# The three remaining slabs of the first x tile in one DMA transpose, ahead of W1's later blocks

## The chip, the cores and the metric

The kernel runs on one core of a Trainium2 chip. The metric is the device time of one execution in microseconds (us), the median of the runs. Before the change it is 212.85 us over 3 runs.

## The reference

Two branches over the same input x (2048 x 640, bf16) are mixed by a gate:

```
g = sigmoid(sum(x * gate_w))                 # one gate for each row
a = 2 * Re(h C^T) + x * Dskip,  h[t] = Lam_bar * h[t-1] + B_bar x[t]   # complex state, 640 wide
b = gelu(x w1 + b1) w2 + b2                  # 640 -> 1728 -> 640
out = g * a + (1 - g) * b
```

The change concerns the first product of branch b alone, x w1, for the first 512 rows of x.

## The kernel before

x is worked on in four tiles of 512 rows. TensorE sums over the partition dimension, so each tile is needed transposed: `xT[q]` holds five slabs of 128 columns of x, each as 128 partitions x 512 rows. W1 lies in `W1sb` as five blocks of 128 rows (block k goes with slab k). Its first 1,024 columns (`FW`, eight groups of 128) are loaded block by block, the other 704 columns for all blocks at once, in two remainders (`w1_r0`, `w1_r1`).

The program isn't written in the order in which it runs. Each piece of work is an `op` with an engine, an estimated duration and latency, and a priority. `Sched.order` then gives every engine a fixed list: at each step it takes, among the items whose inputs are there by the estimates, the one with the lowest priority number. Loads without inputs go to the sync queue (SP) strictly by priority. `Emitter` puts semaphore waits in front of the items that need them.

The start of the kernel, which the change touches, goes like this on the sync queue (priority in brackets):

- `xna0`, `xna1` (0, 0.2): the first two slabs' worth of x, untransposed, 128 KB each. TensorE transposes them through PSUM (L428) and VectorE copies them to slabs 0 and 1 of `xT[0]` (L434).
- W1 block 1 (1) and block 2 (4), 256 KB each (L333, in `load`). Block 0 comes on ScalarE's queue.
- `xtrans(0, 2..2)` (5): slab 2 by a DMA transpose out of x (L340, in `load_T`).
- W1 block 3 (6), `xtrans(0, 3..4)` (7): slabs 3 and 4 in one DMA transpose, W1 block 4 (8).
- the remainders of W1 (20, 21), then the DMA transposes of B (30 to 31.1), of the second x tile (32) and so on.

On TensorE, `m1_first` (L650) makes the product of the first tile with the first 1,024 columns, slab by slab instead of column group by column group, so that it can begin with slab 0 while the others are still on their way. Eight PSUM banks hold the sums. Its order is slab 0 for groups 0 to 6, slab 1 for groups 0 to 6, slab 2 for groups 0 to 6, then the held-back group 7 of slabs 0, 1 and 2, then slabs 3 and 4. A small transpose of the rows of parameters (`cols`, L455) comes between slabs 1 and 2. A matmul of slab k waits for slab k and for block k of W1:

```
                op(f"m1_0_{jf}_{k}_{t0}", "pe", d_mm(t1 - t0), (XK0[k] if h is None else XK0[k][h:h + 1]) + [w1tok(k, jf)], [("bank", jf)],
                   f_mm, prio=pe_prio())
```

All slabs that come by one DMA transpose share one semaphore. Behind `m1_first` follow the rest of the first product (L672, which needs the remainders), the product with B (L715), and the other tiles.

Of the kernel before, what the change touches and what calls it, by code (L numbers as in the profile page):

```python
# [184 lines left out]
def bass_gated_mix__ssm_conv_s5__dense_activation_gelu__prompt_kernel(  # L185
# [22 lines left out]
    KD = D // 128  # L208
# [17 lines left out]
    with ExitStack() as es:  # L226
# [103 lines left out]
        def load(name, eng, sem, dst, src, writes, prio, dur=0.5, lat=2.5, reads=(), after=()):  # L330
            def fn():
                with nc.allow_non_contiguous_dma(reason="columns of small vectors"):
                    return dma_inc(eng, engines[eng].dma_start(dst, src), sem)  # L333
            return op(name, eng, dur, reads, writes, fn, prio=prio, lat=lat, after=after)

        def load_T(name, sem, pairs, writes, prio, dur, lat=3.0, reads=()):
            def fn():
                t = None
                for dst, src in pairs:
                    t = dma_inc("sp", nc.sync.dma_start_transpose(dst, src), sem)  # L340
                return t
            return op(name, "sp", dur, reads, writes, fn, prio=prio, lat=lat)
# [10 lines left out]
        def xtrans(q, ks, prio, dur):  # L353
            load_T(f"xT{q}_{ks[0]}", f"l_xT{q}_{ks[0]}", [(xT[q][:, ks[0]:ks[-1] + 1, :], x2[q * 512:(q + 1) * 512, ks[0] * 128:(ks[-1] + 1) * 128])],
                   [("xT", q, k) for k in ks], prio, dur)
# [3 lines left out]
        def w1load(k, eng, prio, reads=()):  # L359
            edges = [0] + ([WSPLIT[k] * 128] if k in WSPLIT else []) + [FW]  # L360
            for i, (f0, f1) in enumerate(zip(edges, edges[1:])):
                load(f"w1_{k}{i}", eng, f"l_w1{k}{i}", W1sb[:, k, f0:f1], B_w1[k * 128:(k + 1) * 128, f0:f1], [("w1", k, i)], prio=prio + 0.1 * i, lat=2.6, reads=reads)
# [4 lines left out]
        KN = 2  # L367
# [2 lines left out]
            load(f"xna{h}", "sp", f"l_xna{h}", xn[0][:, 2 * h:2 * h + 2, 0:KN * 128],  # L370
                 x2[h * 256:(h + 1) * 256, 0:KN * 128].rearrange("(c p) d -> p c d", p=128), [("xna", h)], 0.2 * h, dur=0.45, lat=2.0 + 0.4 * h)
        w1load(1, "sp", 1)
        w1load(2, "sp", 4)
        xtrans(0, range(2, 3), 5, 1.15)
        w1load(3, "sp", 6)
        xtrans(0, range(3, 5), 7, 1.8)
        w1load(4, "sp", 8)
        FM = FW + 3 * 128
        for i, (f0, f1) in enumerate(((FW, FM), (FM, F))):
            load(f"w1_r{i}", "sp", f"l_w1r{i}", W1sb[:, :, f0:f1], B_w1[:, f0:f1].rearrange("(k p) f -> p k f", p=128), [("w1", "r", i)], prio=20 + i, lat=5.0)  # L380
# [723 lines left out]
```

## Time and profile before

| | us |
|---|---|
| median of 3 runs | 212.85 (212.7 to 212.89) |
| the profiled execution's own time | 212.76 |
| its span, first to last instruction | 211.4 |
| TensorE busy | 207.8 (98% of the span) |
| VectorE busy | 190.1 (90%) |
| ScalarE busy | 103.2 (49%) |

The mean granted TensorE clock is 1.000. All times of instructions are counted from the span's start. PE is a TensorE matmul, PEld a TensorE weight load, DVE VectorE, ACT ScalarE, SP the sync engine, SPq an instruction that its sequencer runs (a DMA issue, whose time is that of the issue, not of the transfer). L340 is line 340 of the kernel. A transfer "lands" when its semaphore has got the full count; the answers on DMA issues give the time from the start of the issue to the landing.

### The profile page before, as it was taken

To read this page: it belongs to the slowest core of one execution; us is meant where nothing else is said; L and a number is where in the kernel's file an instruction comes from. 1 tells how busy PE (TensorE), PEld (TensorE's weight loads), DVE (VectorE), ACT (ScalarE), POOL (GpSimd) and SP (SyncE) were. 2 spreads that over 40 slices of the span, in tenths; PEclk is the share of its full clock that TensorE was granted. 3 is DMA by queue.
4 is the path that set the end of the run, shared out by engine and by line. 5 is a ranking of instruction groups with operands and counts; after the bars stand their busy time and mean duration, and the time that the engine had idled before them with its cause. 6 is when DMAs were issued, how large, how long until landed. Compare 5 with 4: busy or idle time off the path is not lost.

```text
span 211.4 us, 2742 instructions
## 1 busy us (share of the span) xinstructions
PE 207.8 (98%) x1091; PEld 105.3 (50%) x1106; DVE 190.1 (90%) x240; ACT 103.2 (49%) x177; POOL 4.2 (2%) x12
## 2 busy tenths in 40 slices
PE   8999999999999999999999999999999999999996
PEld 4544444444564444444464444444456444567775
DVE  2499999999999999999999999899999999499744
ACT  2399556679850353556680063456660037623330
POOL 1000000120000000000100000000010000000000
DMA  6999899999400020066174000007642000005251
GB/s 177 285 222 152 207 192 249 337 168 222 112 0 3 0 50 0 0 87 147 18 59 115 3 0 0 0 2 77 139 96 112 0 3 0 0 0 105 67 142 62
DMA packets 48504, 19.08 MB, mean 90 GB/s; under 512 B 41452, under 2 KB 47212, under 8 KB 48492
## 3 DMA queue, kind: packets, MB, share of 16 engines
q1 hardware_dynamic: 46688, 17.33, 38.4%
q0 software_dynamic: 1600, 1.32, 4.6%
q10 hardware_dynamic: 204, 0.27, 0.5%
q8 instruction: 8, 0.13, 0.3%
q14 instruction: 4, 0.03, 0.1%
HBM read 8.41 MB, written 2.63 MB: 52 GB/s over the span
## 4 chain that ended last, share of the span: by engine, by line
PE 98%; issue 0%; DVE 0%
PE ps L672 22%; PE ps L715 20%; PE ps L939 20%; PE ps L988 15%; PE ps L802 7%; PE ps L851 5%; PE ps L650 4%; PE ps L416 1%; PE ps L693 1%; PE ps L950 1%; PE ps L428 0%; PE ps L816 0%; DVE W1sb L885 0%; PE ps L441 0%; PE ps L455 0%
## 5 line engine op out<-in xcount | busy, mean ns | idle before, releaser
L672 PE MATMUL ps<-xT,W1sb 128*128 128x512 bf16 x214 | 47.5, 379 | 0.3
L755 DVE TENSOR_TENSOR_SCAN W<-atab,V 128x1280 bf16<-128x1280 f32 x16 | 44.3, 2812 | 0.3
L715 PE MATMUL ps<-xT,BT 128*128 128x512 bf16 x196 | 43.3, 379 | 0.2
L939 PE MATMUL ps<-Gl,W2sb 128*128 128x512 bf16 (+1 forms) x230 | 42.3, 343 | 0.2
L679 ACT ACTIVATE Gl<-ps,cols 128x512 bf16<-128x512 f32 x44 | 29.8, 695 | 15.5 <-PE ps L672 15.5
L672 PEld LDWEIGHTS ps<-xT,W1sb 128*128 128x128 bf16 x220 | 21.5, 98 | 25.9
L988 PE MATMUL ps<-Hb,CT 128*128 128x512 bf16 x150 | 32.9, 379 | 0.0
L939 PEld LDWEIGHTS ps<-Gl,W2sb 128*128 128x128 bf16 x234 | 22.9, 98 | 19.3
L715 PEld LDWEIGHTS ps<-xT,BT 128*128 128x128 bf16 x200 | 19.5, 98 | 23.8 <-ACT Gt L701 0.4
L724 ACT ACTIVATE U<-ps 128x512 bf16<-128x512 f32 x40 | 23.7, 596 | 15.5 <-PE ps L715 15.5
L957 ACT ACTIVATE E1T<-ps,cols 128x512 bf16<-128x512 f32 (+1 forms) x18 | 9.4, 624 | 36.0 <-PE ps L950 36.0
L988 PEld LDWEIGHTS ps<-Hb,CT 128*128 128x128 bf16 x150 | 14.4, 98 | 17.9 <-issue 0.6
L996 ACT ACTIVATE E2T<-ps 128x512 bf16<-128x512 f32 x15 | 9.1, 604 | 13.6 <-PE ps L988 13.6
L802 PE MATMUL ps<-W2sb,Gl 128*128 128x320 bf16 x104 | 14.8, 299 | 0.0
L624 DVE SCALAR_TENSOR_TENSOR trf<-xn,gwb 128x640 bf16<-128x640 bf16 x16 | 13.2, 822 | 0.4
L505 DVE TENSOR_TENSOR V<-V,W 128x1280 bf16<-128x1280 bf16 x16 | 12.5, 821 | 0.3
L505 DVE TENSOR_TENSOR Hb<-Hb,V 128x1280 bf16<-128x1280 bf16 x16 | 12.5, 821 | 0.3
L505 DVE TENSOR_TENSOR V<-mr,U 128x2560 bf16<-128x2560 bf16 x8 | 11.9, 1492 | 0.3
L802 PEld LDWEIGHTS ps<-W2sb,Gl 128*128 128x128 bf16 x104 | 10.1, 98 | 4.3 <-issue 0.3
L505 DVE TENSOR_TENSOR Hb<-c,W 128x2560 bf16<-128x2560 bf16 x8 | 11.9, 1490 | 0.2
L505 DVE TENSOR_TENSOR W<-mi,U 128x2560 bf16<-128x2560 bf16 x8 | 11.9, 1484 | 0.0
L505 DVE TENSOR_TENSOR V<-s,W 128x2560 bf16<-128x2560 bf16 x8 | 11.9, 1484 | 0.0
(93 smaller groups left out, 152.0 us busy)
## 6 DMA issues: line engine op xcount, KB each, us to landing
W2sb<-in_B_w_dram SPq DMA_DIRECT2D x1, 2080.0 KB, 8.7
out_dram<-xn SPq DMA_DIRECT2D x3, 640.0 KB, 4.8
xn<-in_A_x_dram POOLq DMA_DIRECT2D x2, 640.0 KB, 7.4
W1sb<-in_B_w_dram SPq DMA_DIRECT2D x4, 256.0 KB, 4.1
trf<-grow SPq DMA_DIRECT2D x3, 256.0 KB, 5.6
xn<-in_A_x_dram SPq DMA_DIRECT2D x1, 640.0 KB, 7.0
W1sb<-in_B_w_dram SPq DMA_DIRECT2D x1, 480.0 KB, 5.4
out_dram<-W1sb SPq DMA_DIRECT2D x3, 160.0 KB, 1.8
```

The source lines that it names most:

```text
L505: return inc("dve", nc.vector.tensor_tensor(out=o, in0=a, in1=b, op=o_))
L624: t = inc("dve", nc.vector.scalar_tensor_tensor(out=scr[:, :], in0=xn[q % 2][:, c, :], scalar=1.0, in1=gwb[:, :], op0=ALU.mult, op1=ALU.mu ...
L672: t = nc.tensor.matmul(PS[bank][:, :], W1sb[:, k, jf * 128:(jf + 1) * 128], xT[q][:, k, :], start=(k == 0), stop=(k == KD - 1))
L679: return inc("act", nc.scalar.activation(Gl[q % 2][:, jf, :], PS[bank][:, :], ACT.Gelu_apprx_tanh, bias=b1col[:, jf:jf + 1]))
L715: t = nc.tensor.matmul(PS[bank][:, :], BT[:, ci, kd, k * 128:(k + 1) * 128], xT[q][:, kd, :], start=(kd == 0), stop=(kd == KD - 1))
L724: return inc("act", nc.scalar.activation(dst, src, ACT.Copy, scale=1.0 if ci == 0 else -1.0))
L755: t = inc("dve", nc.vector.tensor_tensor_scan(out=g[:, ci, :], data0=a, data1=v[:, ci, :], initial=0.0, op0=ALU.mult, op1=ALU.add))
L802: t = nc.tensor.matmul(PS[bank][:, 0:HALF], Gl[q % 2][:, jf, t4 * 128:(t4 + 1) * 128], W2sb[:, jf, cols], start=False, stop=False, skip_gr ...
L851: t = nc.tensor.matmul(PS[bank][:, 0:n], H[b % NHB][:, ci, k, s * 128:(s + 1) * 128], CT[:, ci, k, cols], start=(i == 0), stop=(i == 2 * K ...
L939: t = nc.tensor.matmul(PS[bank][:, 0:t1 - t0], W2sb[:, jf, d * 128:(d + 1) * 128], Gl[q % 2][:, jf, t0:t1], start=(jf == 0), stop=False)
L957: return inc("act", nc.scalar.activation(E1T[:, d, t0:t1], PS[bank][:, 0:t1 - t0], ACT.Identity, bias=cols2[:, 0, d:d + 1]))
L988: t = nc.tensor.matmul(PS[bank][:, :].rearrange("p (s t) -> p s t", s=2), CT[:, ci, k, d * 128:(d + 1) * 128], Hb[:, 2 * (q % 2):2 * (q % ...
```

## The change

Slabs 2, 3 and 4 of the first x tile come in one DMA transpose with priority 3 (estimated issue 1.4 us), so it stands between W1's block 1 (priority 1) and its block 2 (priority 4). Blocks 2, 3 and 4 keep their priorities 4, 6 and 8 and follow one another. The two DMA transposes of before are gone, and with them one semaphore.

```diff
         w1load(1, "sp", 1)
-        w1load(2, "sp", 4)
-        xtrans(0, range(2, 3), 5, 1.15)
-        w1load(3, "sp", 6)
-        xtrans(0, range(3, 5), 7, 1.8)
-        w1load(4, "sp", 8)
+        xtrans(0, range(2, 5), 3, 1.4)
+        for k in range(KN, KD):
+            w1load(k, "sp", 2 * k)
```

`KN` is 2 and `KD` is 5.

## The prediction

> **What bounds the kernel now.** I read the busy shares, the chain that ended last, the waits of TensorE, the sync queue's timeline at the start, the landings of its transfers, and the DMA rate in short stretches.
>
> The page's busy line and its chain:
>
> ```profile
> PE 207.8 (98%) x1091; PEld 105.3 (50%) x1106; DVE 190.1 (90%) x240; ACT 103.2 (49%) x177; POOL 4.2 (2%) x12
> PE 98%; issue 0%; DVE 0%
> ```
>
> From 3.4 us to 209.45 us the end is set by TensorE alone, matmul behind matmul. The chain around the change, in order of time (start, length, what):
>
> ```profile
> 4.81 0.43 PE ps L428 x4
> 5.24 2.90 PE ps L650 x17
> 8.14 0.06 PE ps L455
> 8.20 2.81 PE ps L650 x13
> ```
>
> No piece waits for a transfer, and in the answer on TensorE's waits the only transfer that a weight load waited for is the x load of L428, 0.5 us at 3.1. So hardly anything can be won on this path: a transfer that lands earlier finds TensorE busy. A transfer that lands too late opens a gap, and that gap comes out at the end in full, since no later idle time takes it up. What counts is the margin of each transfer before its first use. The sync queue's timeline has the issues, and TensorE's first use of slab 2 is the weight load at 7.98:
>
> ```profile
> 1.76 1.05 SPq L333 DMA_DIRECT2D W1sb<-in_B_w_dram  x2
> 2.86 1.25 SPq L340 DMA_TRANSPOSE xT<-in_A_x_dram  x1
> 4.16 0.64 SPq L333 DMA_DIRECT2D W1sb<-in_B_w_dram  x1
> 4.85 1.26 SPq L340 DMA_TRANSPOSE xT<-in_A_x_dram  x1
> 6.15 1.71 SPq L333 DMA_DIRECT2D W1sb<-in_B_w_dram  x3
> ...
> 7.98 5.33 PEld L650 LDWEIGHTS ps<-xT,W1sb 128*128 128x128 bf16 x26
> ```
>
> (The first row is W1's blocks 1 and 2, issued at 1.76 and 2.27; the last x3 is block 4 and the two remainders.) The trace's landings, and the weight load that needs each: block 1 at 6.08, needed 6.25; block 2 at 6.77 and slab 2 at 7.61, both needed 7.98; block 3 at 8.05 and slabs 3 and 4 at 8.95, needed 9.98 (nine steps of 0.216 us after slab 2's second weight load, 8.04); block 4 at 9.61, needed 11.71; first remainder at 12.29, needed 13.43. Margins: 0.17, 1.21, 0.37, 1.93, 1.03, 2.10, 1.14 us.
>
> **The change part by part.** Its own schedule first. The items' order is by priority among those released. With the estimates in the code, slabs 2 to 4 are released to TensorE at 1.40 + 1.4 + 3.0 = 5.8 and block 2 at 3.3 + 2.6 = 5.9, before TensorE gets to slab 2 at about 7.1 there. So by my working the order on TensorE, VectorE and ScalarE stays, and only the sync queue differs.
>
> *The transposes.* Removed: one issue of 1.25 us (one slab) and one of 1.26 (two slabs). Added: one of three slabs, right behind block 1, from 2.27. No row has three slabs. Bounds are the two slabs, 1.26, and the five slabs of a later x tile, 3.00:
>
> ```profile
> 19.38 3.00 SPq L340 DMA_TRANSPOSE xT<-in_A_x_dram  x1
> ...
> L340 SPq DMA_TRANSPOSE BT<-in_A_B_im_dram x2: 1279/2087/2895, 15.1 to 18.1; - x2
> ```
>
> In pieces of 128 elements of a row (256 bytes), 512, 640 and 1,024 pieces took 1.25, 1.28 and 1.26 us, and 2,560 took 2.90 and 3.00. So the price is flat up to 1,024 and not per piece. Read as a staircase, 1,536 more pieces cost two steps of about 0.86; three slabs are 1,536 pieces, one step above the flat: 1.26 + 0.86 = 2.12 us. A straight line between 1,024 and 2,560 would say 1.84. I take 2.12, since the flat part speaks for steps.
>
> The landing of the three: one slab took 4.8 us from issue to landing, the five slabs 5.0, so 7.1 to 7.3 against 7.98. Slab 2 gains margin (0.37 to about 0.7), slabs 3 and 4 more. That is worth nothing in time.
>
> *Block 2 behind them.* This is where the change can cost. Its issue moves from 2.27 to 2.27 + 2.12 + 0.04 (the step between issues) = 4.43, while its first use stays at 7.98. The nearest row is block 3 of before, which goes out at 4.16 and took 3.9 us to land:
>
> ```profile
> W1sb<-in_B_w_dram SPq DMA_DIRECT2D x1, 256.0 KB, 3.9
> ```
>
> It is nearest also by what lies ahead: blocks 1 and 2 and one slab there, block 1 and three slabs now, 640 KB both times. But 256 KB of them are now transposed instead of copied. The rates, in the stretch of slabs 3 and 4 and in that of block 4 (last column GB/s, before it the DMA share):
>
> ```profile
> 6.25:6.50 0.25, 0.25 (x4) 0.13 (x2) 0.00 (x0) 0.00 (x0) 0.00 (x0) 1.00 0.30 55
> 6.50:6.75 0.25, 0.25 (x3) 0.13 (x2) 0.00 (x0) 0.00 (x0) 0.00 (x0) 1.00 1.03 256
> 7.50:7.75 0.25, 0.25 (x2) 0.10 (x1) 0.00 (x0) 0.00 (x0) 0.00 (x0) 1.00 1.28 290
> ...
> 8.50:8.75 0.25, 0.25 (x3) 0.13 (x2) 0.05 (x1) 0.17 (x1) 0.00 (x0) 1.00 1.09 393
> ```
>
> 256 KB at 290 GB/s are 0.90 us and at 393 GB/s 0.67: 0.23 us more. If the delay of the issue and the slower transfers add, block 2 lands at 4.43 + 3.9 + 0.23 = 8.56; if the later issue only uses up time in which the engines were busy anyway, at 8.05 + 0.23 = 8.28. I take 8.48, nearer to the sum, because the stretch 6.25 to 6.50 shows the engines nearly empty (55 GB/s) just before block 3: they waited there for something other than bytes. The lateness is 8.48 - 7.98 = 0.50, and 0.04 from a landing to the weight load (x load landed 3.09, load began 3.13): 0.54, say 0.55 us. Bounds: below, T = 1.26 and block 4's 3.5 us, landing at 7.1, cost 0; a gain is excluded, because TensorE has no gap here that could close. Above, T = 3.00: issue 5.31, landing 9.44, cost 1.5 us.
>
> The Trainium skill, page DMA: Bandwidth & Descriptors, section Latency and other measured facts, gives a DMA transpose with non-contiguous middle dimension an effective 261 GB/s. This trace has 290, and the measurement decides; by 261 the three slabs would take an estimated 1.51 us instead of 1.36 and the cost would be 0.70 instead of 0.55.
>
> *Block 1* keeps its place and issue. Only what follows it changes, transposes instead of block 2, and it has the thinnest margin, 0.17 us. Bounds: no cost, or 0.25 if it slips by one such stretch (0.4 us of emptiness, less the margin). I take 0: nothing ahead of it changes. It doesn't add to block 2's cost either, since a gap at 6.25 moves the need at 7.98 by the same amount.
>
> *Blocks 3 and 4, the remainders, B.* The sync queue's part from 2.27 to B's first transpose at 7.90 loses 1.25 + 1.26 and one step between, and gains 2.12: B goes out about 0.4 earlier. Block 3 goes out near 5.1 and lands by 9.1 (needed 9.98), block 4 near 5.8, landing by 9.8 (11.71); the rest moves forward against margins of over a microsecond. Nothing, unless the queue ahead of them takes over 0.9 us more than I count. The transposes' semaphore of slabs 3 and 4 goes, and with it one wait of TensorE, which never waited: nothing.
>
> The sum: 212.76 us of the profiled execution (span 211.4, and 1.4 around it) + 0.55 = 213.31. The median of the runs is 0.09 above the profiled one: 213.4.
>
> **The rivals.** A difference up to 0.2%, 0.43 us, is about what a measurement here can tell from no change. My forecast (A) is that block 2 lands after 8.37 (7.98 + 0.43 - 0.04): 213.28 to 214.35, by the sum 213.4.
>
> B, not slower: the DMA engines are what block 2 waits for, not the queue. Then its issue at 4.43 or before costs nothing more, it lands at 8.28 or earlier, and the gap is 0.34 us or less: 212.85 to 213.28, middle 213.05. It decides from a landing before 8.37. For it: 640 KB ahead both times, the staircase may be a line (issue at 4.15), and without the emptiness at 6.25 the engines finish 0.3 sooner. Against it: the queue's price of three slabs comes in full before block 2, and the emptiness appears where transposes and copies share the engines, which they still do.
>
> C, faster: TensorE starts the slabs earlier because they land earlier. It needs a wait on them in the profile; there is none, the chain's pieces in this stretch are at most 0.05 us apart. What the end would win is the runs' own spread, 0.1 us: 212.75.
>
> D, block 1 slips instead: 212.85 + 0.25 = 213.1 by the bound above, inside B's range.
>
> **How the numbers follow.** A has 0.57, B and D together 0.37, C 0.06. The likeliest is A, 213.4, its own range 213.28 to 214.35. The range for 8 in 10 goes from 212.85, which leaves out C and the lowest part of B, to 214.2, which leaves out the last of A's bound. Slower by over 0.2%: 0.57; within: 0.38; faster: 0.05 (a part of C is under 0.2%).
>
> **What would show it.** In the changed profile: a transpose of three slabs at 2.27 that takes about 2.1 us (1.84: the line; 1.26: the price is per transfer; 3.0: as for five slabs). Block 2 issued at about 4.4, landing near 8.5. A weight load of L650 that waits for W1's load for some 0.5 us at 8.0, and the same amount at every later piece of the chain. The first remainder matmul, at 13.65 before, would start at about 14.2. I am wrong if the weight load of slab 2 starts at 7.98 as before, if a gap lies at 6.25 or at 10 instead, or if the span moves by another amount than the gap.

## The result, and the profile after

The changed kernel takes 213.81 us (median of 8 runs, 213.44 to 214.24), the kernel before 212.87 us (8 runs on the same chip). The ratio is 1.004, 95% interval 1.003 to 1.005: slower by 0.4%, some 0.9 us. A second set of 11 runs, beside experiments, gave 213.95 us and 1.0046 (1.0032 to 1.006). The profiled execution took 213.92 us, 1.16 us more than the one before; its span is 212.6.

The page's busy line and its chain, after the change:

```profile
PE 208.1 (98%) x1091; PEld 104.6 (49%) x1106; DVE 190.1 (89%) x240; ACT 103.2 (49%) x177; POOL 4.2 (2%) x12
PE 94%; DMA 2%; SPq 2%; issue 1%; DVE 0%
```

TensorE, VectorE and ScalarE do the same work (the traces list the same instructions, by name and shape, in the same sequence), so the busy times stand. What is new is that the chain that ended last has a transfer and the sync queue in it, 2% each. The same chain in order of time (start, length, what) shows where:

```profile
2.27 2.09 SPq L340
4.36 0.05 issue
4.41 4.69 DMA W1sb<-in_B_w_dram
9.10 0.14 issue
9.23 2.96 PE ps L648 x13
```

The line L648 is L650 of before. The chain leads from the transpose's issue (2.09 us) over the issue of W1's block 2 at 4.41 and its landing at 9.10 to slab 2's first matmul. TensorE's weight loads in that stretch, with the idle time ahead of each and what ended it:

```profile
6.50 1.19 PEld L648 LDWEIGHTS ps<-xT,W1sb 128*128 128x128 bf16 x7 [0.39 <-DMA W1sb<-in_B_w_dram]
8.31 0.10 PEld L453 LDWEIGHTS ps<-ident,rows 128*128 128x128 bf16 x1 [0.63 <-issue]
9.20 0.34 PEld L648 LDWEIGHTS ps<-xT,W1sb 128*128 128x128 bf16 x3 [0.79 <-issue]
```

Three waits (the profile puts the last two down to "issue", the engine's own; the landings tell which transfer each waited for): slab 1 starts at 6.50 instead of 6.25, because block 1 landed at 6.45; the transpose of the parameter rows goes at 8.31 instead of 7.76, since the rows' loads landed as late as 8.07; and slab 2 starts at 9.20 instead of 7.98. From there on the shift stays: the first weight load of the remainders 14.63 instead of 13.43, the last matmul ends at 210.63 instead of 209.44. The whole loss, 1.2 us in this execution, is opened by 9.2 us and then carried to the end. The landings, issue by issue (last number: us from issue to landing):

```profile
xT<-in_A_x_dram SPq DMA_TRANSPOSE x1, 6.0
W1sb<-in_B_w_dram SPq DMA_DIRECT2D x1, 256.0 KB, 4.7
```

The three slabs need 6.0 us and land at 8.26, block 2 needs 4.7. Both are late against 7.98. The rate of the DMA engines (last column, GB/s) shows one thing that held them:

```profile
4.25:4.50 0.25, 0.25 (x2) 0.19 (x3) 0.10 (x1) 0.25 (x1) 0.00 (x0) 1.00 0.91 275
...
5.00:5.25 0.25, 0.25 (x7) 0.20 (x3) 0.15 (x1) 0.25 (x1) 0.00 (x0) 1.00 1.36 89
5.25:5.50 0.25, 0.25 (x4) 0.06 (x2) 0.25 (x2) 0.25 (x1) 0.00 (x0) 1.00 0.70 68
...
6.00:6.25 0.25, 0.25 (x4) 0.10 (x1) 0.00 (x0) 0.00 (x0) 0.00 (x0) 1.00 0.30 53
6.25:6.50 0.25, 0.24 (x3) 0.01 (x1) 0.00 (x0) 0.00 (x0) 0.00 (x0) 1.00 1.25 258
```

For more than a microsecond, from 5.0 to 6.25, the engines move 50 to 90 GB/s, where 275 to 290 are usual. Before the change there was one such stretch too, but of some 0.3 us, around 6.25 to 6.50. The trace's single pieces show its nature. Between 4.86 and 4.97 nine of the 256-byte pieces of the transpose begin that normally take 0.018 us; they all end between 6.21 and 6.26. Meanwhile copies of 2 KB, W1's block 1, still run one after the other at 0.084 us each, in two series, the last ending at 6.04. The trace doesn't name the engine of a piece; I take pieces that follow one another without a gap for those of one engine. Each series begins behind a single copy of 2 KB that took far longer: 1.53 us (from 3.95) and 0.71 us (from 4.89). These two copies made their engines late; what held them, no run here tells. Copies of 2 KB that take 0.3 to 1.6 us stand in the first 10 us of every profile of this case, that of the kernel before included. Those engines then do 13 to 16 transposed pieces of their own, and at 6.23 all go on together. I call this a standstill: the transpose's pieces wait for the engines that are behind. No completion of block 1 is counted on any engine before 6.22 either, though most of its copies had ended by 4.9.

### The profile page after: what moved, and what is told of

It reads as the page before. It is cut to its first block, busy times and chain, and to the rows that moved or that the text cites. A ratio compares the mean times of both kernels' runs of the same rounds, so it can differ in the third digit from the quotient of the medians.

```text
span 212.6 us, 2740 instructions
## 1 busy us (share of the span) xinstructions
PE 208.1 (98%) x1091; PEld 104.6 (49%) x1106; DVE 190.1 (89%) x240; ACT 103.2 (49%) x177; POOL 4.2 (2%) x12
## 3 DMA queue, kind: packets, MB, share of 16 engines
q0 software_dynamic: 1600, 1.32, 4.4%
## 4 chain that ended last, share of the span: by engine, by line
PE 94%; DMA 2%; SPq 2%; issue 1%; DVE 0%
PE ps L670 22%; PE ps L713 20%; PE ps L937 20%; PE ps L986 15%; PE ps L800 7%; PE ps L849 5%; PE ps L648 3%; DMA W1sb<-in_B_w_dram 2%; PE ps L691 1%; SPq L340 1%; PE ps L948 1%; SPq L333 1%; PE ps L814 0%; DVE W1sb L883 0%
## 5 line engine op out<-in xcount | busy, mean ns | idle before, releaser
L677 ACT ACTIVATE Gl<-ps,cols 128x512 bf16<-128x512 f32 x44 | 29.8, 693 | 15.5 <-PE ps L670 15.5
```

Source lines behind the costliest of these rows:

```text
L677: return inc("act", nc.scalar.activation(Gl[q % 2][:, jf, :], PS[bank][:, :], ACT.Gelu_apprx_tanh, bias=b1col[:, jf:jf + 1]))
```

## The experiments

The edits are against the changed kernel. Three theories. *Order* (mine): block 2 behind the transposes is late, and the queue's issue time is part of it. *Merge*: one semaphore makes slab 2 wait for slabs 3 and 4. *Standstill*: transposes that begin among copies stop the DMA engines. Some expectations split the first: by the *queue's price* block 2 is late because it is issued later, by the *engines* or *due-bytes* theory because of the bytes ahead of it. *Lockstep* is the standstill's proposed mechanism: a transpose's pieces wait until all engines are through the copies ahead of them.

**Merge alone**, block 2 ahead of it:

```diff
-        xtrans(0, range(2, 5), 3, 1.4)
+        xtrans(0, range(2, 5), 5, 1.4)      # block 1, block 2, slabs 2-4, block 3, block 4
```

> The three slabs come in one DMA transpose as in the change, but behind W1's block 2, where slab 2's transpose stood before (order: block 1, block 2, slabs 2 to 4, block 3, block 4). Order theory (block 2's place behind the transposes costs the time): block 2 is issued at 2.27 again and lands near 6.8, the slabs are issued at 2.86 and land at 7.9 to 8.2, a gap of 0 to 0.3 us at the first weight load of slab 2: 212.9 to 213.2. Merge theory (slab 2 has to wait for all three): the slabs land 6.0 us after their issue as in the changed kernel, at 8.85, a gap of 0.9: 213.75. Standstill theory (the DMA engines stand still when transposes begin among copies): as the merge theory in time, but with the standstill to be seen as a stretch under 100 GB/s.

Measured: 213.55 us, ratio 1.0032 (1.0017 to 1.0046). The transpose's landing, and TensorE's weight loads:

```profile
xT<-in_A_x_dram SPq DMA_TRANSPOSE x1, 6.4
6.88 1.19 PEld L648 LDWEIGHTS ps<-xT,W1sb 128*128 128x128 bf16 x7 [0.88 <-DMA W1sb<-in_B_w_dram]
9.39 0.56 PEld L648 LDWEIGHTS ps<-xT,W1sb 128*128 128x128 bf16 x4
```

Block 2 has its old issue at 2.27 and still the gap is there: the slabs, issued at 2.86, land at 9.26. Block 1, at its old place, lands at 6.83 in this execution, which at 214.11 us is the slowest of the 12 runs; the parameter rows, whose transpose comes ahead of slab 2, land at 9.05, nearly as late as the slabs. My theory's 212.9 to 213.2 is refuted; the merge costs by itself, as the merge and the standstill theories said.

**Order alone**, the two transposes of before, slab 2's ahead of block 2:

```diff
-        xtrans(0, range(2, 5), 3, 1.4)
+        xtrans(0, range(2, 3), 3, 1.15)
+        xtrans(0, range(3, 5), 7, 1.8)      # block 1, slab 2, block 2, block 3, slabs 3-4, block 4
```

> The two DMA transposes stay separate as before the change; only slab 2's goes ahead of W1's block 2 (order: block 1, slab 2, block 2, block 3, slabs 3 and 4, block 4). Order theory: block 2 is issued at 2.27 + 1.25 + 0.05 = 3.57; with the 3.9 us that block 3 took before it lands at 7.5 and nothing is lost, with the 4.7 us that block 2 took in the changed kernel at 8.25 and 0.3 us are lost: 212.9 to 213.2. Merge theory: nothing is lost, 212.87. Standstill theory: the transpose begins among block 1's copies at about 4.4, as in the changed kernel, so the standstill lasts to 6.2 as there, block 1 lands at 6.4 and 0.25 us are lost at least: 213.1 to 213.4.

Measured: 212.67 us, ratio 0.9995 (0.9983 to 1.0007): no difference that can be told. Block 2 went out at 3.55 and landed at 7.95 (fifteen of its 16 parts by 7.17); slab 2 starts at 8.05, 0.07 us later than before:

```profile
W1sb<-in_B_w_dram SPq DMA_DIRECT2D x1, 256.0 KB, 4.4
8.05 1.85 PEld L649 LDWEIGHTS ps<-xT,W1sb 128*128 128x128 bf16 x10 [0.27 <-issue]
```

A transpose ahead of block 2 is thus harmless if it is one slab. A short standstill is there (64 GB/s at 5.25 to 5.50), and block 1 landed at 5.83; the standstill's cost that I expected from it didn't come. A longer one (71 to 85 GB/s from 7.75 to 8.50), around slabs 3 and 4, cost nothing either: they landed at 9.69 and aren't needed before 10.0.

**Split in place**: all three slabs ahead of block 2, but as two transposes.

```diff
-        xtrans(0, range(2, 5), 3, 1.4)
+        xtrans(0, range(2, 3), 3, 1.15)
+        xtrans(0, range(3, 5), 3.5, 1.8)    # block 1, slab 2, slabs 3-4, blocks 2, 3, 4
```

> Slabs 2 to 4 ahead of W1's blocks 2 to 4 as in the change, but as the two DMA transposes of before (order: block 1, slab 2, slabs 3 and 4, blocks 2, 3, 4). Queue's price theory: the two issues take 1.25 + 0.05 + 1.26 instead of 2.09, block 2 goes out at 4.87 instead of 4.41 and lands 0.46 later: 214.2. Engines theory (block 2 waits for the bytes and the standstill ahead of it, not for its issue): as the changed kernel, 213.8. Merge theory: slab 2 lands by itself, but block 2 is still late; 213.6 at best.

Measured: 213.51 us, ratio 1.0032 (1.0018 to 1.0046). The two issues together, and slab 2's first weight load, which waited for block 2:

```profile
2.27 2.63 SPq L340 DMA_TRANSPOSE xT<-in_A_x_dram  x2
8.98 0.99 PEld L649 LDWEIGHTS ps<-xT,W1sb 128*128 128x128 bf16 x6 [0.52 <-issue]
```

Slab 2 lands by itself, at 6.50, and it is block 2 that is late, at 8.88. Block 2 goes out 0.54 us later than in the changed kernel (4.95 against 4.41) and its last part lands no later (8.88 against 9.10). That alone doesn't clear the issue: in the changed kernel fifteen of the 16 parts landed at 8.50 to 8.63 and one at 9.10, here all 16 at 8.78 to 8.88, so most parts did come later with the later issue. One thing moved beside the edit: TensorE went on to the held-back group 7 (weight load at 8.37) ahead of slab 2, not behind it, since the schedule reckoned block 2 as later. One matmul of 0.21 us (at 8.38) filled part of the wait, so that this run understates the loss by as much. Without that it would be about 213.7, the changed kernel's time and below the 214.2 of the queue's price theory. By the time, then, the later issue costs nothing more; by the landings this isn't settled.

**Block 2 on ScalarE's queue**, clear of the transpose's issue:

```diff
-        for k in range(KN, KD):
+        for k in range(KN + 1, KD):
             w1load(k, "sp", 2 * k)
...
         w1load(0, "act", -110, reads=["rz"])
+        w1load(2, "act", -105, reads=["rz"])
```

> As the changed kernel, but W1's block 2 is issued by ScalarE's queue right behind block 0, ahead of the parameter rows, so it waits for no transpose's issue. Order theory: block 2 lands at 5 to 6 us, far ahead of its first use at 7.98; what is left is the slabs' landing (8.26 in the changed kernel) and block 1's (6.45): 0.2 to 0.4 us, 213.1 to 213.3. If the standstill alone is what costs: block 1 and the slabs are as late as in the changed kernel or later, because block 2 shares the engines with them; block 1 at 6.8 and slabs at 8.7, 213.6 or more.

Measured: 213.4 us, ratio 1.0032 (1.0019 to 1.0046). Block 2 was issued at 1.41 and landed at 5.72, over two microseconds ahead of its use. The loss moved to others, in TensorE's waits:

```profile
PEld ps L427 <- DMA xn<-in_A_x_dram: 1.2, 2, 0.7
PEld ps L454 <- issue: 0.4, 1, 0.4
```

The second half of x for slabs 0 and 1 landed at 5.01 instead of 4.21 (fifteen of its 16 parts by 4.38), and the parameter rows at 8.03. The slabs landed at 7.84, in time. Taking the later issue away thus wins nothing that can be told from the changed kernel. I read it so: what has to come through the engines before 8 us is too much, and somebody is late.

**Dose: two slabs ahead of block 2.**

```diff
-        xtrans(0, range(2, 5), 3, 1.4)
+        xtrans(0, range(2, 4), 3, 1.4)
+        xtrans(0, range(4, 5), 7, 1.15)     # block 1, slabs 2-3, block 2, block 3, slab 4, block 4
```

> Slabs 2 and 3 in one DMA transpose ahead of W1's block 2, slab 4 alone ahead of block 4 (order: block 1, slabs 2 and 3, block 2, block 3, slab 4, block 4). Two slabs took the queue as long as one (1.26 and 1.25 us). Queue's price theory: block 2 goes out at 3.57 as with slab 2 alone ahead, and nothing is lost: 212.7. Due-bytes theory (everything ahead of the last transfer that slab 2's first matmul needs has to pass the 16 DMA engines by 7.98): 128 KB more than with slab 2 alone, 0.45 us at 290 GB/s, block 2 lands at 8.4 instead of 7.95: 213.0 to 213.2, halfway to the changed kernel.

> The order with slabs 2 and 3 ahead of block 2 once more, since its first interval left it open whether it loses anything: due-bytes theory 213.0 to 213.2 (0.2 to 0.4 us over the kernel before), queue's price theory no difference.

Measured: 213.11 us, ratio 1.0011 (0.9998 to 1.0024), and again 213.25 us, 1.0013 (1.0 to 1.0027). The issue took 1.32 and 1.35 us and block 2 went out at 3.64 and 3.67, nearly as with one slab. With one, two and three slabs ahead of block 2 the ratios are 0.9995, 1.0011 to 1.0013, and 1.0032 to 1.0046. The middle one's intervals just touch 1, so the step from none is likely, not certain; the series of ratios goes with the bytes, 128 KB each, and not with the issue time. The profiles don't show the step's cause. Block 2 landed at 7.48 in the first and 8.11 in the second, and in neither did TensorE wait for it: in the second slab 2 starts at 8.50 because the matmuls before it ran at half pace for longer, to 6.6 us (see the last section).

**Without the parameter rows' loads**, to see whether small pieces make an engine late:

```diff
-            return inc("pool", nc.gpsimd.memset(rows[:, :], 0.0))
+            return inc("pool", nc.gpsimd.memset(rows[:, :], -0.5))
...
-            load(nm, "act", "l_" + nm, rows[r0:r0 + src.shape[0], :], src, [nm], prio=-100 + i, dur=0.4)
...                                          # the load of b1b, two lines, goes too
+            pass
```

> The changed kernel without the five small loads of the parameter rows on ScalarE's queue (the rows are set to -0.5 in SBUF instead, so the parameters and with them the output are others). If the small pieces make one DMA engine late, which the transposes then wait for: no or a short standstill, block 2 lands by 8.2, 212.9 to 213.2. If they are not the cause: as the changed kernel, 213.6 to 213.9.

Measured: 213.9 us, ratio 1.0053 (1.0029 to 1.0078), as the changed kernel. The standstill stays; two stretches of it:

```profile
5.25:5.50 0.25, 0.25 (x4) 0.19 (x2) 0.25 (x2) 0.00 (x0) 0.00 (x0) 1.00 0.60 111
5.50:5.75 0.25, 0.25 (x3) 0.19 (x2) 0.21 (x1) 0.00 (x0) 0.00 (x0) 1.00 0.38 83
```

The rows aren't the cause of the standstill: three copies of 2 KB that take 1.07 to 1.18 us, from 3.8 to 4.0, are there without them.

**The changed kernel again**, as reference:

> The changed kernel again, as the reference for the others of this call and for a second profile: 213.5 to 213.9. By the lockstep theory the length of the standstill follows the latest engine and differs from run to run, with the landing of block 2 between 8.4 and 9.2; if it is a fixed price, block 2 lands at 9.1 again.

Measured: 213.95 us, as given above. The standstill was milder (120 to 190 GB/s from 4.50 to 5.75), block 1 landed at 5.86 and the slabs at 7.91, both in time, yet block 2 landed at 9.20, 4.7 us after its issue at 4.47. In these two profiles and in that without the rows' loads it landed at 9.10, 9.20 and 9.23; the last of its 16 parts came 0.45 to 0.48 us behind the fifteenth (8.63, 8.72, 8.78). I had expected landings that follow the standstill; they do not. In the first profile the pieces tell why the last part is late: on its engine one 2 KB copy of block 2 took 1.02 us (7.23 to 8.26) instead of 0.084, with the standstill long over. The second has copies of 0.99 and 0.67 us in the same stretch (from 6.82 and 7.52), but which of them held the last part isn't followed here. What makes single copies slow stays open.

**The transpose without copies ahead.** The sync queue waits for block 1 before it issues the transpose.

```diff
+                if name == "xT0_2":
+                    nc.sync.wait_ge(sems["l_w110"], 16)
                 for dst, src in pairs:
```

> The changed kernel, but the sync queue waits until W1's block 1 has landed before it issues the DMA transpose of the three slabs, so no copy of that queue is in flight when the transpose's pieces start. It is late by design: block 1 lands near 6, the transpose is issued at 6.1, block 2 at 8.2, so some 4 us are lost, 216 to 217. What it is for is the transpose by itself. Lockstep theory (the pieces of a DMA transpose wait until every engine has come through the copies ahead of them): no standstill, no transposed piece of over 0.3 us, 1,536 pieces through in 1.4 to 1.6 us at 290 GB/s, landing 4.0 to 4.3 us after the issue instead of 6.0. Rival (a large transpose stands still at its start by itself): a stretch under 100 GB/s of about a microsecond also here, landing 5 to 6 us after the issue.

Measured, in a single run: 215.93 us. The issue, the landing, and the rate:

```profile
5.51 1.49 SPq L342 DMA_TRANSPOSE xT<-in_A_x_dram  x1
xT<-in_A_x_dram SPq DMA_TRANSPOSE x1, 3.7
7.00:7.25 0.25, 0.25 (x3) 0.10 (x1) 0.00 (x0) 0.00 (x0) 0.00 (x0) 1.00 1.05 245
7.50:7.75 0.25, 0.25 (x3) 0.10 (x2) 0.00 (x0) 0.00 (x0) 0.00 (x0) 1.00 0.80 180
8.25:8.50 0.25, 0.15 (x2) 0.00 (x0) 0.07 (x1) 0.00 (x0) 0.00 (x0) 1.00 1.30 294
```

No standstill once the pieces run, none of them over 0.15 us, and 3.7 us from issue to landing instead of 6.0. A large transpose doesn't stand still by itself; it does behind copies. And its issue takes 1.49 us here, not 2.09.

**Three engines made late on purpose**: as the last one, with two loads of 3 rows of 20 KB ahead of the transpose.

```diff
                     nc.sync.wait_ge(sems["l_w110"], 16)
+                    for i in range(2):                    # 3 rows of 20 KB into Hb, written over later
...                                                       # n, dst and src of the load
+                        late_eng.append(dma_inc("sp", nc.sync.dma_start(dst, src), "l_late"))
```

> As the kernel that waits for block 1 before the transpose, with two more loads right ahead of the transpose on the same queue: 3 rows of 20 KB each, so that they occupy few of the 16 DMA engines, for about 0.9 us each (2 KB took 0.084 us on an engine). The loaded values are written over later, unread. Lockstep theory: after the first dozen pieces on each engine all transposed pieces stand still until the late engines have come through, over a microsecond at under 100 GB/s with pieces of 0.5 us and more, and the transpose lands that much later than 3.7 us after its issue. Independent engines: the other engines go on through their pieces at their own pace, 13 of 16 parts of 290 GB/s, and only the late engines' pieces come behind; no transposed piece of over 0.3 us.

Measured, in a single run: 217.77 us, the transpose 4.3 us from issue to landing.

```profile
7.75:8.00 0.25, 0.25 (x3) 0.01 (x1) 0.00 (x0) 0.00 (x0) 0.00 (x0) 1.00 0.80 182
8.25:8.50 0.25, 0.00 (x0) 0.00 (x0) 0.07 (x1) 0.15 (x1) 0.00 (x0) 1.00 1.49 41
8.50:8.75 0.25, 0.00 (x0) 0.00 (x0) 0.16 (x2) 0.06 (x1) 0.00 (x0) 1.00 0.36 14
9.00:9.25 0.25, 0.00 (x0) 0.00 (x0) 0.21 (x2) 0.23 (x2) 0.00 (x0) 1.00 1.28 292
```

Copies on three engines stop the transpose on all of them, at 14 to 41 GB/s; 21 pieces of 0.3 us and more end together, between 8.86 and 8.90, just ahead of the second load's completions at 8.96 to 9.00. That speaks for lockstep and against independent engines. A gap is left in it: the trace holds the first load's pieces alone (the last ends at 7.75), and that the second load kept its engines until the pieces went on is read from its completions. The size was off: the standstill is 0.6 us and not over a microsecond, and some 520 pieces had gone through before its end, not a dozen on each engine. The 217.77 us hold more than the late transpose, since TensorE ran at half pace for a while after its wait (last section).

## Why the prediction was right or wrong

*What bounds the kernel*: right. TensorE had no wait to lose and none was won; the gap at the start came out at the end in full.

*The issue of three slabs*: 2.12 us forecast, 2.09 measured, and block 2's issue at 4.43 forecast, 4.41 measured. But the reasoning, a staircase in the number of pieces, is not borne out: the same transpose issued in 1.49 us with no copies ahead and 1.65 with the two late loads ahead, and in 1.84 to 2.25 in the other kernels. The rows from which I read steps were rows of a loaded queue. So the number was right by luck.

*The landing of the slabs*: 7.1 to 7.3 forecast, 8.26 and 7.91 measured. This step failed; it put the 4.8 and 5.0 us of other transposes on this one, whose first pieces stood still for up to 1.37 us. In the first profile the slabs alone would have cost 0.3 us, which I had counted as nothing.

*Block 2*: the mis-sized term of the sum. 8.48 forecast, 9.10 and 9.20 measured, so 1.2 us were lost in the profiled execution where I had 0.55, and 0.9 in the median. I took block 3's 3.9 us and 0.23 for the slower transposed bytes; it was 4.7. The standstill of 0.3 us, which I saw in the rates of before and carried along as part of the 3.9, grew to over a microsecond in that profile, and the last of block 2's 16 parts came nearly 0.5 us behind the others. Most parts met the forecast: fifteen landed at 8.50 to 8.63 in the first profile, twelve at 7.94 to 8.11 in the second. What the sum had no term for is that one late part of 16 holds up all, and that a single slow copy makes a part late.

*Queue or engines*: here the reasoning was half wrong. I set the queue's issue price (A) against the engines (B), with the engines as the case that costs nothing. Merge alone and block 2 on ScalarE's queue lose 0.3% with no later issue of block 2, so the engines cost that much by themselves; split in place, no slower for an issue 0.54 us later, points the same way. How much the later issue adds in the changed kernel isn't shown. B's argument, 640 KB ahead both times, compared block 2 with block 3 and forgot that block 3 had until 9.98. What counts, as I read these runs, is what must be through by 7.98: block 1, block 2 and one slab before, and two slabs more now, whether they stand in front of block 2 or share slab 2's semaphore.

*Block 1*: taken as 0, with 0.25 as its bound (D). It cost 0.24 in one profile and nothing in the other, and didn't add to block 2's gap, as forecast.

*The rest* (blocks 3 and 4, remainders, B, the order on the compute engines): right, no wait on any of them. *C, faster*: excluded, as argued.

No order tried here beats the kernel before by more than can be told; slab 2 alone ahead of block 2 equals it (0.9983 to 1.0007).

## What to carry to other kernels

For each transfer at the start, add up the bytes that have to come through before its first use, by everything ahead of it in the queue and everything that shares its semaphore; merging a transfer that is due with two that aren't makes all of them due. A DMA transpose that begins behind unfinished copies stood still here until the most belated DMA engine was through, so its price is not what it takes alone (3.7 us; 6.0 behind copies). The landing of a transfer is that of its last part: look at the parts before explaining it. Read a thin margin in the profile, here 0.17, 0.37 and 1.21 us, as what the next change has to spend, and don't trust one landing: it moved by half a microsecond and more between profiles of the same order.

## What the runs showed of the hardware that I had not expected

Transposed pieces waited for one another across the DMA engines, as told above. The Trainium skill, page DMA: Bandwidth & Descriptors, section Rules for kernel authors, says that a transpose next to ordinary DMAs needs nothing. That sentence is about the data; in time it cost the stretches at 50 to 90 GB/s here.

TensorE's pace doubled at a moment that differs from run to run. A matmul over 256 columns follows the one before after 0.21 us at first and after 0.11 later; the change came between 4.4 us (slab 2 alone ahead) and 6.8 us (without the rows' loads). The granted clock in the profile's rows reads 1.00 on both sides, but that says little: six of the twelve traces hold no record of the clock, the other six have one that begins at the doubling (4.75 in the changed kernel, 4.32 with slab 2 alone ahead), and where there is none the rows read 1.00. With three engines late the record shows the halving too: after TensorE had stood idle for some 3 us ahead of slab 2, the granted clock was 0.50 from 12.1 to 15.5 us, with 0.43 us for 512 columns instead of 0.216. The skill's page TensorE: Matmul & The Clock Gate, section Part 1: The HAM clock gate, speaks of a free-running window of 3.4 us and of a transition that varies by half a microsecond either way; the runs agree in kind and show a wider spread, 2.4 us. It moves the moment at which block 1 is needed (5.87 to 6.98 us among the profiles without a wait for it) and block 2 (7.91 and 8.50 in the two profiles with two slabs ahead), and can be part of the spread of about 1.4 us in the runs of the kernel before, 212.19 to 213.56; how much of it, no run here tells.
